# A fused linear-attention and MLP kernel: seven uneven MLP tiles (3, 4, 4, 4, 4, 3, 2) in place of six tiles of four, with an interleaved attention opening

## The chip, the cores and the metric

The kernel runs on one core of one Trainium2 chip. The metric is device time in microseconds (us) of one execution. An execution has a span (first to last instruction of the profile) and a measured time, which is 1.7 to 2.4 us longer than the span. A profile is one execution, so a few tenths of a us in it mean little; the medians of the timed runs decide.

Engine names: PE is TensorE (matmul), DVE is VectorE, ACT is ScalarE, POOL is GpSimd, SP is SyncE. POOL issues the loads, which also cast from 32-bit to 16-bit floats; SP issues the transposes that are done by DMA, and the stores.

## The reference, cut to what matters

There are 4 batches, 8 heads, 768 positions and head size 64. Decayed linear attention feeds an MLP with an ELU activation (512 to 2048 to 512) over 3072 tokens.

```python
# per batch and head, blocks of the sequence in order (lam: one decay per head)
intra = ((qb @ kb.T) * Dmask) @ vb              # Dmask[i,j] = lam**(i-j) for i >= j, else 0
inter = (qb * lam_pow) @ kv_state
out   = intra + inter
kv_state = lam**block * kv_state + (kb * rev_pow).T @ vb
# then, on x = out as [3072, 512]
h = x @ w_in                                    # 512 -> 2048
g = where(h > 0, h, exp(min(h, 0)) - 1)
y = g @ w_out                                   # 2048 -> 512
```

## The kernel before

The reference goes in blocks of 64 positions; the kernel, which computes the same sums, uses blocks of 128 tokens, called chunks here: 24 chunks, numbered 0 to 23, six for each batch. A *tile* is the set of chunks that go through the MLP together: four chunks, 512 tokens. A tile takes 16 *slots*, one for each 128 of the 2048 features: `mm1` gives 128 features for the tile's tokens, ACT and DVE make the ELU, and two slots later `mm2` adds the slot into one PSUM bank for each chunk. Slots are numbered through the whole kernel, so slot 16 is the first one of the second tile.

The attention of the chunks of the next tile is spread over the slots of the current one. Each chunk needs its queries and keys transposed, to have the head size on partitions. Chunks 0 to 3 have nothing to hide behind: their attention runs before slot 0, and they are transposed on PE; all later chunks are transposed by DMA.

```python
CPT = 4                                   # chunks in a tile
def att_T_dma(g):                         # transposes by DMA, issued on SP
    qt = asb.tile([128, NHP, 128], FP16, tag="qT", bufs=3, ...)
    z = asb.tile([128, NHP, 2, 128], FP16, tag="kz", bufs=3, ...)
    nc.sync.dma_start_transpose(out=qt[:], in_=...)        # queries
    nc.sync.dma_start_transpose(out=z[:]..., in_=kn[g % NB]...)   # keys, padded with zeros
def att_T_pe(g):                          # transposes on PE, only for chunks 0 to 3
    pt = ps.tile([128, 2, NHP, 128], FP16, tag="psH", bufs=2, ...)
    ...
def mm1(s):
    pH = ps.tile([128, MT], FP32, tag="psH", bufs=2, ...)
    for kk in range(NHP):
        nc.tensor.matmul(pH[:], lhsT=wi[:, kk, ...], rhs=xt[m][:, kk, :], ...)
    nc.scalar.activation(e[:], pH[:], AF.Exp)
    nc.scalar.activation(r[:], pH[:], AF.Relu)
def elu(s, e, r):                         # DVE, two inputs in SBUF
    nc.vector.scalar_tensor_tensor(out=g[:], in0=e[:], scalar=-1.0, in1=r[:], op0=ALU.add, op1=ALU.min)
def F(g):                                 # the slot in which chunk g's attention starts
    t, c = divmod(g, CPT)
    return 2 + 3 * c if t == 1 else (t - 1) * NFT - 2 + 4 * c
...
    if g < 2 * CPT:                       # chunks 4 to 7
        prep.append((f - 4, lambda g=g: att_T_dma(g)))
        prep.append((f - 1, lambda g=g: att_kd(g)))
    else:                                 # POOL scales q and k, then the transposes
        prep.append((f - 6, lambda g=g: (att_q(g), att_kd(g), att_T_dma(g))))
...
for g in range(CPT):                      # opening: chunk after chunk
    att_T_pe(g); att_ev(g); ...
    for hp in range(NHP):
        att_SU(g, hp)                     # scores and state, one bank for a pair of heads
        att_P(g, hp)                      # times the mask
    ...
```

Names in the profile: `psH` is the result of `mm1`, `psM` are the banks of `mm2`, `psSU` the scores, `psT` the PE transposes; `qn`, `kf`, `kn` and `vz` are the loaded queries, keys, zero-padded keys and values; `qT` and `kz` are transposed queries and keys; `kd` are decayed keys, `st` the state, `osb` the output before its store, `wi` and `wo` the weight slices.

## Time and profile before

| | before |
|---|---|
| time, median of 3 | 249.99 us (248.77 to 250.59) |
| span of the profile | 248.6 us |
| first `mm1` (slot 0) | 38.0 us |
| first `mm1` of the second tile (slot 16) | 79.5 us |
| last `mm1` to the end | 9.3 us |

The first lines of the profile page give the span, and the busy share of each engine in tenths, in 40 equal slices of 6.2 us. PEclk is the granted TensorE clock in tenths of full speed.

```profile
span 248.6 us, 3981 instructions
PE   0256658989697999999999999999999999999991
PEclk9999765999889999999999999999999999999999
```

From the 14th slice to the last but one PE is 90% busy or more. There is little to win there unless PE gets less to do. The loss is in the first 80 us and the last 10. The list of PE's waits (engine, what was to start, what released it: total, times, longest, in us) says what it waited for.

```profile
...
PE psH_507 L346 <- DVE xt_312 L333: 2.3, 1, 2.3
PE psSU_0_837 L270 <- DMA kz_692<-kn_92: 2.3, 1, 2.3
```

Those above them are waits for the first load and within the opening. The first shown is the end of the opening, at slot 0. The second is in the first tile: chunk 7's scores wait for its keys, transposed by DMA. The timeline (start, duration, engine, line, what; in brackets the idle time before and its releaser) has both, and the first `mm1` of slot 16 and the last of all.

```profile
38.01 1.87 PE L346 MATMUL psH_507<-xt_312,wi_0_127 128*128 128x512 f16 x4 [2.33 <-DVE xt_312 L333]
66.41 0.28 PE L270 MATMUL psSU_0_837<-qT_691,kz_692 128*128 128x128 f16 x2 [2.26 <-DMA kz_692<-kn_92]
79.52 1.03 PE L346 MATMUL psH_991<-xt_672,wi_0_127 128*128 128x512 f16 x4
239.26 1.03 PE L346 MATMUL psH_3072<-xt_2493,wi_4_131 128*128 128x512 f16 x4
```

How long a DMA transpose takes from issue to landing, in the last column, is told by the view of DMA issues: the keys of chunk 4, the first that is transposed by DMA, and those of chunk 7, which PE waited for.

```profile
kz_499<-kn_89 SPq DMA_TRANSPOSE x1, 10.5
...
kz_692<-kn_92 SPq DMA_TRANSPOSE x1, 8.9
```

And the chain of waits, followed back from the end, shows what leads to chunk 7's wait (start, duration, what).

```profile
19.62 8.68 DMA wi_2_129<-in_moe_w_in_dram
28.59 17.55 DMA qn_187<-in_q_dram
46.42 10.98 DMA kn_92<-in_k_dram
57.49 8.87 DMA kz_692<-kn_92
```

### The profile page before, as it was taken

The numbers are of one execution on the slowest core, as the hardware profiler recorded it, in microseconds if no ns is written. First come the engines' busy times: TensorE is split into PE (matmuls) and PEld (weight loads), VectorE is DVE, ScalarE is ACT, GpSimd is POOL, SyncE is SP. The second block draws the span as 40 slices with busy tenths as digits, with TensorE's granted clock in tenths as the row PEclk, the third lists the DMA queues.
The fourth block names the chain that finished last, engine by engine and source line by source line (L and its number), as shares of the span: only waits on it lengthen the run. The fifth ranks groups of instructions, "written<-read, shape, count | busy, mean of one in ns | idle before, by whom it ended". The sixth has DMA issues, their size and how long they took to land.

```text
span 248.6 us, 3981 instructions
## 1 busy us (share of the span) xinstructions
PE 215.2 (87%) x1344; PEld 113.0 (45%) x1344; DVE 166.2 (67%) x378; ACT 141.7 (57%) x307; POOL 117.0 (47%) x141
## 2 busy tenths in 40 slices
PE   0256658989697999999999999999999999999991
PEld 0144433545254455555555554555555555444440
DVE  8447764777468988665888987557888765444342
ACT  2794443545433756667666567576675665755651
POOL 7997534538999987802689868012400000000000
PEclk9999765999889999999999999999999999999999
DMA  6999999999999999982999999943227000040004
GB/s 43 125 151 182 191 112 192 169 176 124 149 151 158 129 262 159 88 84 52 179 171 143 123 104 127 177 83 63 44 70 186 3 0 1 0 171 0 0 0 169
DMA packets 115588, 28.05 MB, mean 113 GB/s; under 512 B 107888, under 2 KB 112496, under 8 KB 115568
## 3 DMA queue, kind: packets, MB, share of 16 engines
q0 software_dynamic: 79968, 13.64, 82.0%
q1 hardware_dynamic: 35600, 14.17, 31.2%
q8 instruction: 10, 0.16, 0.3%
q14 instruction: 10, 0.08, 0.1%
HBM read 27.27 MB, written 6.29 MB: 135 GB/s over the span
## 4 chain that ended last, share of the span: by engine, by line
PE 65%; DMA 19%; POOL 7%; DVE 3%; issue 2%; ACT 1%; DVEq 0%; SPq 0%; ACTq 0%; POOLq 0%
DMA qn_187<-in_q_dram 7%; DMA kn_92<-in_k_dram 4%; DMA kz_692<-kn_92 4%; DMA wi_2_129<-in_moe_w_in_dram 3%; PE psM_3_1558 L372 1%; PE psM_1_2506 L372 1%; PE psM_1_1556 L372 1%; PE psM_3_2508 L372 1%; PE psM_2_1557 L372 1%; PE psM_2_2507 L372 1%; PE psM_3_2042 L372 1%; PE psM_1_2040 L372 1%; PE psM_3_1087 L372 1%; PE psM_1_1085 L372 1%; PE psM_0_2505 L372 1%
## 5 line engine op out<-in xcount | busy, mean ns | idle before, releaser
L346 PEld LDWEIGHTS <-wi_4_131 128*128 128x128 f16 x96 | 9.4, 100 | 10.8 <-issue 1.1
L346 PEld LDWEIGHTS <-wi_3_130 128*128 128x128 f16 x96 | 9.2, 98 | 10.1
L346 PEld LDWEIGHTS <-wi_2_129 128*128 128x128 f16 x96 | 9.1, 98 | 9.9
L346 PEld LDWEIGHTS <-wi_0_127 128*128 128x128 f16 x48 | 4.9, 106 | 7.9 <-issue 4.1
L346 PEld LDWEIGHTS <-wi_1_128 128*128 128x128 f16 x48 | 4.9, 102 | 7.2 <-issue 2.5
L101 POOL DMA_DIRECT2D kn_91<-in_k_dram x6 | 4.5, 757 | 5.8 <-DMA qn_180<-in_q_dram 3.5
L101 POOL DMA_DIRECT2D kn_92<-in_k_dram x6 | 4.5, 757 | 4.4 <-DMA wo_3_135<-in_moe_w_out_dram 2.5
L212 POOL TENSOR_TENSOR kd_2298<-kn_90,ks 128x512 f16<-128x512 f16 x1 | 1.0, 1045 | 11.4 <-PE psSU_3_2225 L275 11.4
L212 POOL TENSOR_TENSOR kd_1591<-kn_92,ks 128x512 f16<-128x512 f16 x1 | 1.0, 1045 | 10.8 <-PE psSU_3_1501 L275 10.8
L246 PE MATMUL psT_221<-ident_141,qn_137 128*128 128x128 f16 x4 | 0.6, 308 | 4.9 <-DMA qn_137<-in_q_dram 4.9
L101 POOL DMA_DIRECT2D kn_90<-in_k_dram x6 | 4.5, 757 | 0.6 <-DMA wo_1_133<-in_moe_w_out_dram 0.4
L270 PEld LDWEIGHTS <-kz_0_93 128*128 128x128 f16 x16 | 1.6, 116 | 7.1 <-ACT kz_0_93 L257 7.1
L101 POOL DMA_DIRECT2D kn_89<-in_k_dram x6 | 4.6, 798 | 0.0
L270 PEld LDWEIGHTS <-kz_1_94 128*128 128x128 f16 x16 | 1.7, 120 | 5.3 <-ACT kz_1_94 L257 5.3
L101 POOL DMA_DIRECT2D vz_77<-in_v_dram x3 | 2.7, 900 | 2.8 <-DMA wo_4_136<-in_moe_w_out_dram 2.8
L270 PE MATMUL psSU_0_248<-qT_230,kz_0_93 128*128 128x128 f16 x2 | 0.6, 288 | 4.0 <-ACT kz_0_93 L257 4.0
L351 ACT ACTIVATE e_512<-psH_507 128x512 f32<-128x512 f32 x1 | 0.6, 597 | 5.9 <-PE psH_507 L346 5.9
L346 PE MATMUL psH_507<-xt_312,wi_0_127 128*128 128x512 f16 x4 | 1.9, 622 | 2.3 <-DVE xt_312 L333 2.3
L317 PEld LDWEIGHTS <-vz_83 128*128 128x128 f16 x24 | 2.4, 102 | 3.2 <-issue 0.6
L212 POOL TENSOR_TENSOR kd_2411<-kn_91,ks 128x512 f16<-128x512 f16 x1 | 1.0, 1045 | 5.7 <-issue 5.7
L317 PEld LDWEIGHTS <-vz_82 128*128 128x128 f16 x24 | 2.4, 98 | 2.8
L317 PEld LDWEIGHTS <-vz_81 128*128 128x128 f16 x24 | 2.3, 98 | 2.8
(1647 smaller groups left out, 851.0 us busy)
## 6 DMA issues: line engine op xcount, KB each, us to landing
wi_2_129<-in_moe_w_in_dram POOLq DMA_DIRECT2D x1, 512.0 KB, 8.7
wo_2_134<-in_moe_w_out_dram POOLq DMA_DIRECT2D x1, 512.0 KB, 10.7
wi_3_130<-in_moe_w_in_dram POOLq DMA_DIRECT2D x1, 512.0 KB, 14.0
wo_3_135<-in_moe_w_out_dram POOLq DMA_DIRECT2D x1, 512.0 KB, 16.6
wi_4_131<-in_moe_w_in_dram POOLq DMA_DIRECT2D x1, 512.0 KB, 12.5
wo_4_136<-in_moe_w_out_dram POOLq DMA_DIRECT2D x1, 512.0 KB, 15.0
vz_77<-in_v_dram POOLq DMA_DIRECT2D x3, 128.0 KB, 7.1
vz_78<-in_v_dram POOLq DMA_DIRECT2D x3, 128.0 KB, 5.5
```

What stands on the lines that cost most here:

```text
L101: nc.gpsimd.dma_start(out=dst, in_=src[:, rows].rearrange("h p d -> p h d"))
L212: eng.tensor_tensor(out=kd[:].rearrange("p (g t) d -> p g t d", t=2), in0=nats[g][1], in1=ks[:].rearrange("p (g t) -> p g t", t=2).unsquee ...
L246: nc.tensor.transpose(pt[:, j, hp, :], in_=src[:, 2 * hp : 2 * hp + 2, :], identity=ident16[:])
L270: nc.tensor.matmul(pu[:, hh * 128 : (hh + 1) * 128], lhsT=z[:, hp, hh, :], rhs=qt[:, hp, :], start=True, stop=True,)
L317: nc.tensor.matmul(po[:, hp, :], lhsT=vt[:, b0 : b0 + 2, :], rhs=P[:, hh, :], start=(hh == 0), stop=(hh == 1 and cb == 0), skip_group_chec ...
L346: nc.tensor.matmul(pH[:], lhsT=wi[:, kk, j * 128 : (j + 1) * 128], rhs=xt[m][:, kk, :], start=(kk == 0), stop=(kk == NHP - 1),)
L351: nc.scalar.activation(e[:], pH[:], AF.Exp)
L372: nc.tensor.matmul(psM[m][i][:], lhsT=g[:, i * 128 : (i + 1) * 128], rhs=wo16[wof[n][0]][:, wof[n][1], :], start=(n == 0), stop=(n == NFT ...
```

## The change

The intent is to start the MLP earlier and to end it sooner. The first tile has three chunks, so one chunk less is to be computed before slot 0; the last has two, so the last activations and stores are shorter. The opening's attention is interleaved: transposes of the next chunk, scores of this one and outputs of the last stand beside each other, four heads share a score bank, and the mask multiplication takes four heads at once. Zeroing is moved behind the front of the opening. Chunks 3 to 6, whose attention runs in the first tile, are transposed on PE. The DMA transposes of chunks 4 to 6 leave the queues. The weights come in eight slices of two slots in place of 2, 2, 4, 4, 4, and the order of the loads is another: chunk 7's load stood behind the last weight slice and now stands before slice 4 (slices are numbered from 0).

```diff
-    CPT = 4
-    MT = CPT * L
-    NMT = (B * S) // MT
+    TILES = [3, 4, 4, 4, 4, 3, 2]
+    NMT = len(TILES)
+    MTMAX = max(TILES) * L
+    T0 = [sum(TILES[:i]) for i in range(NMT + 1)]
+    G1 = T0[1]
+    G2 = T0[2]
...
-    WG = [2, 2, 4, 4, 4]
+    WG = [2] * 8
...
+    for g, (ft, f) in zip(range(G1, G2), ((-1, 1), (3, 5), (7, 9))):
+        at(ft, lambda g=g: (att_T_pe(g), att_ev(g)))       # chunks 3, 4, 5: on PE
+        regular(g, f)
+        prep.append((f - 1, lambda g=g: att_kd(g, nc.vector)))
+    at(12, lambda: (att_T_pe(G2 - 1), att_ev(G2 - 1)))      # chunk 6
+    short(G2 - 1, 13)
+    START = {4: (-2, 4), 3: (0, 5), 2: (2, 6)}              # first slot and step by tile size
+    for t in range(2, NMT):
+        off, step = START[TILES[t]]
+        for c in range(TILES[t]):
+            g, f = T0[t] + c, (t - 1) * NFT + off + step * c
+            regular(g, f)
+            prep.append((f - 6, lambda g=g: (att_q(g), att_kd(g, nc.gpsimd), att_T_dma(g))))
+            prep.append((f - 16, lambda g=g: emit_load(g)))
...
-    for g in range(CPT):
-        att_T_pe(g)
-        att_ev(g)
-        ...
+    att_T_pe(0)
+    att_ev(0)
+    late_zeros()
+    att_T_pe(1)
+    SU(0)
+    att_kd(0, nc.scalar)
+    ...
+    att_ev(1)
+    att_T_pe(2)
+    SU(1)
+    ...
```

A consequence: the chunks of the first two tiles have their queries scaled by DVE when the attention output is written, and these tiles now end at chunk 6. So chunk 7, the first of the third tile, is now the first to have its queries and keys scaled by POOL, and the first to be transposed by DMA. Its attention starts in slot 14.

## The prediction

> **What bounds it now.** From about 80 us on, TensorE does: the chain of waits shows one mm1 group (four matmuls, 0.86 us) every 2.06 us while attention is interleaved, every 1.73 us in the last tile, PE 100% busy in the windows. So one chunk-slot of the MLP (a 128-token chunk, one of 16 feature slots) costs 1.73/4 = 0.43 us and an attention chunk 4 x 0.33 = 1.3 us of PE. Their sum does not change. Losses are at the ends. Opening: the first mm1 starts at 38.0 us (timeline), after a serial attention of four chunks (first scores at 10.7, 17.3, 24.2, 31.2). Tile 0: slots 0 to 16 take 38.0 to 79.7 = 41.7 us; the PE sum is 16 x 1.73 + 4.5 x 1.3 = 33.5. The rest is a cold clock (windows: 0.50 from 33 to 42 us), a 2.3 us wait for the DMA-transposed keys of chunk 7 (landed 66.4 us, 8.9 after issue), a cold clock again, and 1 us waits on the one score bank. A cold clock after a gap is what the Trainium skill says (TensorE: Matmul & The Clock Gate, Part 1). Tail: last mm1 at 239.3, end 248.6.
>
> **What the change does.**
> 1. Opening: one chunk less (about 6.9 us), interleaved, wider masks (0.69 us for four heads instead of 2 x 0.42), DVE zeroing off the front. Adding durations on DVE (13 us of work after the first transposed copy at about 9 us) and ACT (15 us) gives the first mm1 at 25.5 us (24 to 28).
> 2. Tile 0 has three chunks: 16 x 1.29 = 21 us, attention of four chunks (5), eight PE transposes for each (0.45 warm): 28 us warm, 30 with a cold start.
> 3. PE transposes free the DMA queues of 1.2 MB in the opening and take 8 to 10 us of latency off chunks 3 to 6. Weight slices land in time by my sum (the queue moved 145 GB/s on q/k/v, 200 on weights): slice 4 at 37, slice 7 at 48 us.
> 4. New wait: chunk 7 is now the first with a DMA transpose, needed in slot 14, about 52 us. On POOL its q scaling stands behind the loads of chunks 8 and 9, whose issue waits for slice 7 (eight loads outstanding). So the transposes issue at about 50 us and land at 57 to 59: PE waits some 6 us and restarts cold. Slot 16 starts about 63 us instead of 79.7.
> 5. After slot 16: 21 instead of 20 chunks of MLP (+6.9), one more attention chunk (+1.3), one more tile change (+0.6), tail with two chunks (shorter activations, two stores instead of four: -2.1): 168.9 + 6.7 = 175.6 us.
>
> **Sum.** Span 63 + 175.6 = 238.6; timed runs are 1.4 us above: **240.0 us**, range 234.5 to 244.5. Chances: faster by over 2% 0.93, within 2% 0.06, slower 0.01.
>
> **What would show it.** First mm1 near 25.5 us; slots of 1.75 us in tile 0; a PE wait of 4 to 8 us for the transposed keys of chunk 7 near 52 to 58 us, then a clock of 0.5; slot 16 near 63; last mm1 to end 7.2 us instead of 9.3; 2.06 us unchanged in full tiles.
>
> **What would make it wrong.** No wait for chunk 7 (shorter transpose latency): 233 to 235 us. Weights or chunk 6 late in tile 0, or chunk 7's load held by the zeroing of its key buffer, which ACT does last in the opening: 243 us or more. In the last tiles ACT or the two activation banks could bind at 0.86 us a slot.

## The result, and the profile after

The changed kernel gives correct results and takes 243.67 us (median of 4, 243.32 to 243.78) against 249.73 of the kernel before. The ratio is 0.976, with a 95% interval of 0.972 to 0.979. Ratios here are the mean time of one kernel's runs over that of the other's runs of the same rounds, so they are not quite the ratio of the medians that are quoted. Executions over 1.5% slower than the fastest of the same kernel are left out of the means. The change is faster by 2.4%. The predicted 240.0 was 3.7 us too low; the time lies within the range.

| profile | before | predicted | after |
|---|---|---|---|
| span | 248.6 | 238.6 | 241.3 |
| slot 0, first `mm1` | 38.0 | 25.5 | 25.8 |
| wait for chunk 7's keys | 2.3 | about 6 | 5.9 |
| slot 16, first `mm1` | 79.5 | 63 | 64.4 |
| from there to the end | 169.1 | 175.6 | 176.9 |
| last `mm1` to the end | 9.3 | 7.2 | 6.8 |

The first lines of the page, after; a slice is 6.0 us.

```profile
span 241.3 us, 4272 instructions
PE   1377799960989999999999999999999999999992
PEclk9999999996799999999999999999999999999999
```

PE is busy much earlier, but has a hole in the tenth slice, and the clock is low after it. PE's waits, after, name the hole: the same wait for chunk 7's keys as before, 2.6 times as long.

```profile
PE psSU_0_885 L333 <- DMA kz_671<-kn_92: 5.9, 1, 5.9
...
PE psT_217 L260 <- DMA qn_151<-in_q_dram: 2.9, 1, 2.9
...
PE psM_1_1026 L436 <- DVE osb_1_990 L444: 1.1, 1, 1.1
```

The timeline, after: slot 0, the end of the wait, the `mm1` of slot 15 at half the clock (1.49 us, where that of slot 14, of the same width, took 0.81), slot 16, and the last `mm1`.

```profile
25.79 0.81 PE L409 MATMUL psH_442<-xt_302,wi_0_118 128*128 128x384 f16 x4
59.87 0.39 PE L333 MATMUL psSU_0_885<-qT_670,kz_671 128*128 128x128 f16 x2 [5.88 <-DMA kz_671<-kn_92]
61.44 1.49 PE L409 MATMUL psH_898<-xt_302,wi_7_125 128*128 128x384 f16 x4
64.39 1.03 PE L409 MATMUL psH_937<-xt_583,wi_0_118 128*128 128x512 f16 x4
234.51 0.60 PE L409 MATMUL psH_3280<-xt_2905,wi_7_125 128*128 128x256 f16 x4
```

In the view by stretches (stretch; length; busy time of PE, PEld, DVE, ACT, POOL; then the granted clock, the DMA share and GB/s) the clock falls during the wait and stays at 0.50 to about 63 us. The Trainium skill, page "TensorE: Matmul & The Clock Gate", Part 1, says that the clock is half after about one idle window of 3.4 us, and comes back after about as long a busy one. This trace agrees in the return: PE is busy again from 59.87 us, and in stretches of 0.5 us the clock is 0.50 up to 63.0 and 1.00 from 63.5. The fall came sooner than that: PE's last matmul before the wait ended at 54.0 us, and the clock is 0.93 in the stretch from 56.0 and 0.50 from 56.5, so it fell after some 2.4 us.

```profile
54.00:57.00 3.00, 0.00 (x0) 0.00 (x0) 0.62 (x2) 1.14 (x6) 3.00 (x5) 0.90 1.24 113
57.00:60.00 3.00, 0.13 (x2) 0.13 (x3) 0.00 (x0) 0.00 (x0) 3.00 (x4) 0.50 2.23 155
60.00:63.00 3.00, 3.00 (x13) 1.50 (x12) 1.45 (x4) 0.00 (x0) 3.00 (x4) 0.50 1.35 144
```

Why were the keys late? The chain of waits, after, has it (most pieces are left out; nearly all of them are loads that POOL issues).

```profile
26.18 8.80 DMA vz_82<-in_v_dram
...
41.25 8.73 DMA wo_7_133<-in_moe_w_out_dram
50.02 0.49 issue
50.51 0.88 POOL vz_78 L108
51.41 1.06 POOL qn_409 L233
52.47 1.00 POOL kd_668 L225
...
53.88 5.95 DMA kz_671<-kn_92
```

POOL's work stands in the trace in the order of the program. Its scaling of chunk 7's queries (`qn_409`) stands behind the loads of chunks 8 and 9, and the last of those (`vz_78`) waited for the last weight slice (`wo_7`, issued at 41.25) to land; the late loads in this trace each wait for the landing of the load eight places before them. Only then come the scaling, the decayed keys, and the transposes on SP. So up to about 60 us the chain of the kernel after is mostly its queue of loads, as that of the kernel before was.

### The profile page after: what moved, and what is told of

It reads as the page before. It is cut to its first block, busy times and chain, and to the rows that moved or that the text cites. A ratio compares the mean times of both kernels' runs of the same rounds, so it can differ in the third digit from the quotient of the medians.

```text
span 241.3 us, 4272 instructions
## 1 busy us (share of the span) xinstructions
PE 212.7 (88%) x1444; PEld 120.5 (50%) x1444; DVE 164.8 (68%) x381; ACT 147.6 (61%) x335; POOL 121.1 (50%) x146
## 4 chain that ended last, share of the span: by engine, by line
PE 67%; DMA 13%; POOL 10%; DVE 5%; issue 3%; ACT 1%; SPq 0%; DVEq 0%; ACTq 0%; POOLq 0%
DMA vz_82<-in_v_dram 4%; DMA wo_7_133<-in_moe_w_out_dram 4%; DMA wo_1_127<-in_moe_w_out_dram 4%; DMA kz_671<-kn_92 2%; PE psM_3_1503 L436 1%; PE psM_1_1026 L436 1%; PE psM_1_2416 L436 1%; PE psM_3_2418 L436 1%; PE psM_1_1501 L436 1%; PE psM_2_1502 L436 1%; PE psM_2_2417 L436 1%; PE psM_2_1027 L436 1%; PE psM_0_1500 L436 1%; PE psM_3_1028 L436 1%; PE psM_0_2415 L436 1%
## 5 line engine op out<-in xcount | busy, mean ns | idle before, releaser
L409 PEld LDWEIGHTS <-wi_7_125 128*128 128x128 f16 x56 | 5.7, 102 | 6.3 <-issue 0.9
L409 PEld LDWEIGHTS <-wi_1_119 128*128 128x128 f16 x56 | 5.3, 97 | 6.7 <-issue 2.1
L409 PEld LDWEIGHTS <-wi_3_121 128*128 128x128 f16 x56 | 5.4, 98 | 5.3
L409 PEld LDWEIGHTS <-wi_5_123 128*128 128x128 f16 x56 | 5.4, 98 | 5.3
L409 PEld LDWEIGHTS <-wi_4_122 128*128 128x128 f16 x56 | 5.4, 98 | 5.0
L409 PEld LDWEIGHTS <-wi_2_120 128*128 128x128 f16 x56 | 5.3, 98 | 4.8
L409 PEld LDWEIGHTS <-wi_6_124 128*128 128x128 f16 x56 | 5.3, 98 | 4.8
L409 PEld LDWEIGHTS <-wi_0_118 128*128 128x128 f16 x56 | 5.3, 98 | 4.7
L414 ACT ACTIVATE e_903<-psH_898 128x384 f32<-128x384 f32 x1 | 0.5, 490 | 7.8 <-PE psH_898 L409 7.8
L108 POOL DMA_DIRECT2D kn_92<-in_k_dram x6 | 4.5, 764 | 0.8 <-DMA wi_2_120<-in_moe_w_in_dram 0.6
L374 PEld LDWEIGHTS <-vz_79 128*128 128x128 f16 x24 | 2.6, 112 | 2.8 <-issue 0.9
L333 PEld LDWEIGHTS <-kz_671 128*128 128x128 f16 x8 | 0.7, 114 | 6.1 <-DMA kz_671<-kn_92 6.1
L374 PEld LDWEIGHTS <-vz_84 128*128 128x128 f16 x24 | 2.3, 98 | 2.8 <-DVE xt_583 L395 0.5
L374 PEld LDWEIGHTS <-vz_81 128*128 128x128 f16 x24 | 2.3, 98 | 2.5
L374 PEld LDWEIGHTS <-vz_80 128*128 128x128 f16 x24 | 2.3, 98 | 2.5
L374 PEld LDWEIGHTS <-vz_82 128*128 128x128 f16 x24 | 2.3, 98 | 2.5
```

The costliest lines, as they stand in the source:

```text
L108: nc.gpsimd.dma_start(out=dst, in_=src[:, rows].rearrange("h p d -> p h d"))
L333: nc.tensor.matmul(pu[:, hh * 128 : (hh + 1) * 128], lhsT=z[:, hp, hh, :], rhs=qt[:, hp, :], start=True, stop=True,)
L374: nc.tensor.matmul(po[:, hp, :], lhsT=vt[:, b0 : b0 + 2, :], rhs=P[:, hh, :], start=(hh == 0), stop=(hh == 1 and cb == 0), skip_group_chec ...
L409: nc.tensor.matmul(pH[:, :w], lhsT=wi[:, kk, j * 128 : (j + 1) * 128], rhs=xt[m][:, kk, :w], start=(kk == 0), stop=(kk == NHP - 1),)
L414: nc.scalar.activation(e[:, :w], pH[:, :w], AF.Exp)
```

## The experiments

Each was run beside the kernel before on the same chip, on four chips. "After" is the changed kernel; diffs are against it. Slot 16 is the start of its first `mm1`. Twelve kernels ran; all gave correct results.

The theory is that (1) the wait for chunk 7's transposes, which stands at the end of POOL's queue of loads, hides most of what the opening wins; (2) taking the transposes of chunks 3 to 6 off the DMA queues is the largest part of the gain; (3) the short last tile is worth some 2 us; (4) the eight weight slices are worth little. The main rival is that the earlier opening itself is the gain, and chunk 7's wait just one wait among several. The experiments test one part of it, the interleaving; the other part, that one chunk less stands before slot 0, was never undone alone.

### 0. The changed kernel again (after_again)

No edit.

> Control: the changed kernel, unedited, on the chip of this call. Both theories: 243.7 us as before (243.3 to 244.1), PE wait of 5.9 us for the DMA-transposed keys of chunk 7.

Measured: 243.43 us (243.35 to 244.4), ratio 0.975 (0.972 to 0.979), span 241.3. The median repeats to 0.1%. But the six runs of one kernel can lie 3 us apart (oldopen below), so a difference of 1 us between medians is at the limit of what can be read.

### 1. Chunk 7's scaling and transposes early (early7)

```diff
-            prep.append((f - 6, lambda g=g: (att_q(g), att_kd(g, nc.gpsimd), att_T_dma(g))))
+            at_q = 1.5 if g == G2 else f - 6          # chunk 7: in slot 2 instead of 8
+            prep.append((at_q, lambda g=g: (att_q(g), att_kd(g, nc.gpsimd), att_T_dma(g))))
```

Chunk 7 also gets its own buffers for `qT` and `kd`, so that the early work waits for no buffer.

> Edit: chunk 7's q scaling, decayed keys and DMA transposes are recorded before the loads of chunks 8 and 9 (own buffers), so POOL reaches them at about 42 us instead of 51.4. Theory (the 5.9 us wait comes from POOL's program order, and the cold restart after it costs about 1.6 us more): keys of chunk 7 land at about 50 to 52, the wait in slot 14 (54 us) is gone; but chunk 8's transposes keep their place (issue 57.8, landing 64.6) and are needed at about 62 us, so some 2 to 3 us of wait come back there: 238 to 240 us. Rival A (the keys only hide another limit of tile 0, such as DVE, ACT or the load queue): under 2 us gained, 242 or more.

Measured: 241.84 us (241.15 to 242.75), ratio 0.969 (0.965 to 0.972), span 239.8. Slot 16 starts at 58.5 us, 5.9 earlier than after, as the theory wants. But the time fell by only 1.8 us. PE's waits between 56 and 72 us tell where the rest went.

```profile
PE psSU L335 <- DMA kz<-kn: 3.4, 1, 3.4
```

This wait ends at 66.8 us and is chunk 8's: its transposes were issued at 58.4 and 59.7 us, at about the same time as in the kernel after (57.8 and 59.1), while PE now needs them some 6 us sooner. The wait was moved on to the next chunk. The expected size was a miss.

### 2. The same, and the loads behind it in a better order (early7_ord)

```diff
-            prep.append((f - 16, lambda g=g: emit_load(g)))
+            prep.append((-2 if g == G2 else f - 13, lambda g=g: emit_load(g)))
```

The edit of early7 stays in. The loads of chunk 8 and later are recorded three slots later, so that POOL's scaling no longer stands behind the loads of the chunks after.

> Edit: as early7, and the loads from chunk 8 on are recorded three slots later, so that each chunk's q scaling on POOL stands before the load of the chunk two further. Theory: the wait moves to nothing: about 7.5 us less than the changed kernel, 236 us (235 to 237.5), no PE wait over 1.5 us between 30 and 70 us, clock 1.0 there. Rival A: 241 or more. Rival B (the whole gain was had by early7): same time as early7 within 0.5 us.

Measured: 237.93 us (236.82 to 239.38), ratio 0.953 (0.949 to 0.957), span 234.7. Slot 16 is at 57.9 us, and from there to the end it takes 176.8 us, the 176.9 of the kernel after. (The profiled run was the fastest of the six, 236.82 us.) No wait for a transpose is left. So the chunk 7 wait, with the order of POOL's queue that makes it, costs the changed kernel 243.67 - 237.93 = 5.7 us (5.5 against after_again on the same chip): nearly as much as the whole change had won. That part of the theory is shown.

It was 1.9 us above the expectation. The timeline of DVE around 40 us shows a new loss: the ELU instruction `g`, which takes 0.56 us, takes 2.86.

```profile
38.93 0.56 DVE L424 SCALAR_TENSOR_TENSOR g<-e,r 128x384 f16<-128x384 f32 x1
40.54 2.86 DVE L424 SCALAR_TENSOR_TENSOR g<-e,r 128x384 f16<-128x384 f32 x1
```

The timeline of POOL shows what ran meanwhile: the two multiplications for chunk 7.

```profile
40.92 1.06 POOL L234 TENSOR_TENSOR qn<-qn,qp 128x512 f16<-128x512 f16 x1
41.92 1.05 POOL L226 TENSOR_TENSOR kd<-kn,ks 128x512 f16<-128x512 f16 x1
```

The Trainium skill, page "SBUF — State Buffer", section "Who interferes with whom", says: "A DVE instruction with two SBUF inputs contends with a GpSimd instruction that reads SBUF". `g` has two SBUF inputs, and both POOL multiplications read SBUF; the trace agrees, with 2.86 us for 0.56. The time from slot 9's `mm1` to slot 10's is 3.14 us here and 1.58 in the kernel after. Experiment 5 tests it.

### 3. The old opening in the changed kernel (oldopen)

The opening is written as in the kernel before, chunk after chunk with a score bank for a pair of heads, but for three chunks; all else is as after.

```diff
+    for g in range(G1):
+        att_T_pe(g)
+        att_ev(g)
+        ...
+        att_kd(g, nc.scalar)
+        ...
+        if g > 0:
+            PIs(g - 1)
+            att_X(g - 1)
+        pu = [old_S(g, hp) for hp in range(NHP)]
+        for hp in range(NHP):
+            old_st(g, hp, pu[hp])
```

> Edit: only the opening undone: chunks 0 to 2 one after the other with one narrow score bank per head pair, all else as changed. Theory (the first mm1 is off the critical path, because the wait for chunk 7's keys absorbs it): first mm1 about 4 to 5 us later (30 to 31 us), slot 14 reached at about 58 instead of 54, the wait for chunk 7 about 2 us instead of 5.9, time within 1 us of the changed kernel (243 to 245). Rival C (an earlier first mm1 is worth its full time): 4 to 5 us slower, 248 us.

Measured: 242.1 us (240.34 to 243.48), ratio 0.969 (0.964 to 0.974), span 239.1; the intervals of this ratio and of the changed kernel's overlap. So the interleaved opening gains nothing that can be seen in the changed kernel. The six runs fall into two groups, 240.3 to 241.1 and 243.1 to 243.5 us, and the profile is of the faster one; why is open. In it the `mm1` of slot 0 starts 2.5 us later (28.25 against 25.79; the line shown holds slots 0 and 1), yet slot 16 comes 2 us sooner, at 62.4.

```profile
28.25 2.76 PE L402 MATMUL psH<-xt,wi 128*128 128x384 f16 x8
...
59.51 0.28 PE L326 MATMUL psSU<-qT,kz 128*128 128x128 f16 x2 [0.67 <-DMA kz<-kn]
```

Chunk 7's keys land at nearly the same time whichever opening is used (the wait ends at 59.51 us, after at 59.87). PE arrives there later, so it waits 0.67 us in place of 5.88, and the clock is not as low for as long: 0.77 and 0.66 in the stretches from 54 to 60 us, and 1.00 from 60 on, where the kernel after has 0.50 to 63 us. Here an earlier start by interleaving only meant waiting longer and restarting cold.

### 4. Old opening, with the wait taken away (oldopen_early7_ord)

The edits of 2 and 3 together.

> Edit: the old serial opening (as in oldopen) together with early7_ord, so without the wait for chunk 7's keys. In oldopen the first mm1 came only 2.4 us later than in the changed kernel, and the time did not grow. Theory (the opening counts once nothing behind it waits): 2 to 2.5 us slower than early7_ord, 240 us. Rival D (tile 0 is paced by the load queue in any case, so the opening never counts): within 0.5 us of early7_ord, 238 us.

Measured: 240.89 us (239.5 to 240.94), ratio 0.965 (0.962 to 0.968), span 237.6, slot 16 at 60.2 us. Beside early7_ord this is 3.0 us slower in the medians, 2.3 us in slot 16's start, and the ratios' intervals are apart. So the interleaved opening is worth 2 to 3 us as soon as the wait for chunk 7 is gone, and nothing that can be seen before. As far as the interleaving goes, the rival falls. It stays open for the larger part of the earlier start: with the old way of writing the opening, slot 0 is still at 28.25 us and not at 38.0, because one chunk less stands before it (and zeroing is moved).

### 5. Chunk 7 without POOL's arithmetic (c7raw)

Chunk 7 is treated like chunks 3 to 6: its queries are scaled when the attention output is evicted by DVE, its keys are decayed on DVE. Its load moves back, from before weight slice 4 to behind slice 5 (in front of chunk 6's), and its transposes are by DMA, early.

```diff
-            if g < G2:
+            if g <= G2:
...
+            if g == G2:
+                prep.append((1.5, lambda g=g: att_T_dma(g)))
+                prep.append((f - 1, lambda g=g: att_kd(g, nc.vector)))
+                continue
...
+        (-2, lambda: emit_load(G2)),          # before weight slice 6
```

The later loads are recorded at f - 13, as in early7_ord.

> Edit: chunk 7's q is not scaled on POOL but, like chunks 0 to 6, at the product's eviction on DVE; its decayed keys are made on DVE; its load stands after slice 5; later loads as in early7_ord. So POOL does no tensor work before chunk 8. In early7_ord one g instruction on DVE (two SBUF inputs) took 2.86 us instead of 0.56, just while POOL did its two multiplications at 40.9 to 43.0 us, and slots 9 to 10 took 3.1 us instead of 1.6. Theory F (DVE and POOL wait for each other at the SBUF port; the skill says so for a DVE instruction with two SBUF inputs): no g over 1.3 us before 50 us, slot 16 near 56 us instead of 57.9, 236 us (235 to 237). Rival G (the long slot is the weight queue's doing): slots 9 to 10 stay at 3 us, 237.5 or more.

Measured: 239.11 us (238.96 to 239.93), ratio 0.960 (0.957 to 0.962), span 238.1: a miss, 1.2 us slower than early7_ord in the medians (the intervals of the ratios just touch). On the disputed point it was plain: with no POOL arithmetic there, the `g` at the same place takes its usual time.

```profile
40.32 0.56 DVE L423 SCALAR_TENSOR_TENSOR g<-e,r 128x384 f16<-128x384 f32 x1
```

Slots 9 to 10 take 1.58 us again. So POOL's multiplications did stretch it. But the moved load and the transposes now stand beside the load of chunk 6, and PE waits for that one twice. PE's waits for DMA from 26 to 75 us (the last is for chunk 8's transposes, at 66.4 us):

```profile
PE psT L261 <- DMA kf<-in_k_dram: 1.8, 1, 1.8
PE psSU L340 <- DMA vz<-in_v_dram: 1.2, 1, 1.2
PE psSU L334 <- DMA kz<-kn: 1.0, 1, 1.0
```

In early7_ord PE waits for no DMA in this stretch. These 4 us are more than the 1.6 us that were won.

### 6. Another plan of tiles, ending with four (tail4)

```diff
-    TILES = [3, 4, 4, 4, 4, 3, 2]
+    TILES = [3, 4, 3, 3, 3, 4, 4]
```

This was meant to measure the short last tile alone.

> Edit: only TILES, to [3,4,3,3,3,4,4]: seven tiles and the same work, but the last tile has four chunks as before the change. Theory (a two-chunk tail saves what its shorter activations and two fewer stores save): last mm1 to the end 9.3 us instead of 6.8, 2.5 us slower than the changed kernel: 245.9 us (245 to 247). Rival H (the size of the last tile only moves work about): within 0.7 us of 243.5.

Measured: 239.94 us (239.27 to 240.63), ratio 0.962 (0.960 to 0.965), span 237.8. It was to be slower and was 3.7 us faster. The end is slower, as expected: 9.6 us from the last `mm1` to the end, against 6.8. But the third tile now has three chunks, and in the change's own table of starts (`START`) a tile of three begins its attention at slot 16 and not at 14. That moves chunk 7's preparation two slots later, and the loads of chunks 8 and 9 three and four: its transposes are issued at 49.7 and 51.1 us, before chunk 9's load, in place of 52.5 and 53.9, and they are needed later. The wait for chunk 7 is gone. The edit changed two things, so as a measure of the tail it failed; it is a second, unplanned sign of what the wait costs, though the plan changes later tiles as well.

### 7. The same third tile, with a short end (tiles343)

```diff
-    TILES = [3, 4, 4, 4, 4, 3, 2]
+    TILES = [3, 4, 3, 4, 4, 4, 2]
```

> Edit: only TILES, to [3,4,3,4,4,4,2]. As in tail4 the third tile has three chunks, so chunk 7 is needed in slot 16 instead of 14 and its scaling on POOL stands before the load of chunk 9; the last tile has two chunks as in the changed kernel. In tail4 this took the wait for chunk 7 away (slot 16 at 54.7 us instead of 64.4), which hid what its four-chunk tail cost (last mm1 to the end 9.6 us in the trace, 6.8 in the changed kernel). Theory: tail4's 239.9 less 2.8 us: 237.1 us (236.3 to 238.2). Rival H (the size of the last tile only moves work about): 239.9 within 0.7 us.

Measured: 237.61 us (236.93 to 238.51), ratio 0.952 (0.948 to 0.956), span 236.0. Against tail4 this is 2.3 us, and in the profiles the time from the last `mm1` to the end is 7.05 us against 9.6. So the two-chunk end is worth about 2.3 us, as the prediction had it (2.1). The two plans differ in the middle tiles too, so the 2.55 us between the ends in the profiles are the cleaner figure. The line of a list of seven numbers gives as much as the reordering of experiment 2.

### 8. Chunks 3 to 6 transposed by DMA again (dmaT, dmaT2)

```diff
-        at(ft, lambda g=g: (att_T_pe(g), att_ev(g)))
+        prep.append((f - 4, lambda g=g: att_T_dma(g)))
...
-    at(12, lambda: (att_T_pe(G2 - 1), att_ev(G2 - 1)))
+    prep.append((7.5, lambda: att_T_dma(G2 - 1)))       # dmaT: 9
```

The keys of these chunks are loaded into the zero-padded form, in two halves each. This undoes more than the change did: chunk 3 was transposed on PE before, too, and four more loads stand in POOL's queue.

> Edit: only the PE transposes of chunks 3 to 6 undone: they are transposed by DMA again, four slots ahead, everything else as changed. Theory (the PE transposes pay by taking 1.5 MB and their latency out of the load queue): chunk 3's keys land near 31 us instead of being ready at 27; slice 7 lands 6 to 8 us later, and with it chunk 7's transposes at about 66 us; time about 6 to 7 us more than the changed kernel, 250 us (247 to 252). Rival I (they were hidden, prepared four slots ahead): within 1 us of 243.5.

Measured for dmaT: 259.15 us (257.17 to 259.7), ratio 1.038 (1.034 to 1.042). This edit was flawed: chunk 6's transposes were recorded behind chunk 7's on SP, which waits for POOL, and PE waited 14.5 us for them. The mended one puts them ahead.

> Edit: as dmaT, with its slip mended: there chunk 6's DMA transposes stood behind chunk 7's on the one issuing queue, which waited for POOL, and PE waited 14.5 us for them. Now they stand before. Theory (the PE transposes pay by taking 1.5 MB and 8 to 10 us of latency out of the opening): waits of 5.8 us for chunk 3 and about 3 us for chunk 5 stay, slice 7 and so chunk 7's transposes come 6 to 8 us later than in the changed kernel: 250 us (247 to 253). Rival I (hidden): within 1.5 us of 243.5.

Measured for dmaT2: 254.75 us (252.8 to 256.45), ratio 1.021 (1.016 to 1.026), span 252.9, 11.1 us slower than after. From slot 16 on it takes 176.8 us as ever; the loss is all before it (slot 16 at 76.1 us in place of 64.4). PE's waits:

```profile
PE psSU L335 <- DMA kz<-kn: 14.2, 5, 7.0
...
PE psH L411 <- DMA wi<-in_moe_w_in_dram: 2.6, 1, 2.6
```

The transposes are late five times (for chunks 3 to 7: 1.8, 0.8, 3.1, 7.0 and 1.5 us), and a weight slice once. The last weight slice was issued at 50.6 us against 41.3 after, and POOL's scaling of chunk 7 came at 60.7 against 51.4: the loads are held back too, by the transposes, by the split key loads or by both. On PE, eight transposes of a warm chunk took 0.45 us (39.46 to 39.91 us in the kernel after). So transposing chunks 3 to 6 on PE is worth 11 us in the changed kernel, the largest effect of any experiment; with DMA it is slower than the kernel before (by a ratio of 1.021). What the change's own part of it is worth, chunks 4 to 6 and with the same key loads, was not measured apart.

### 9. The old weight slices (slices5)

```diff
-    WG = [2] * 8
+    WG = [2, 2, 4, 4, 4]
```

> Edit: only the weight slices undone, to five of 2, 2, 4, 4, 4 feature groups, in the same order among the loads. Theory (at most eight loads are outstanding, and slices land some 2 us before their slot): the same bytes in fewer and larger loads, slices 4 to 7 not waited for; time within 1 us of the changed kernel's 243.5, the wait for chunk 7's keys still 5 to 7 us. Rival J (smaller slices let the MLP start on a half-landed slice): a PE wait for a slice of 2 us or more in slots 4 to 12, and 2 us or more slower.

Measured: 242.39 us (241.22 to 243.38), ratio 0.971 (0.967 to 0.975), span 240.8. PE waited for no slice, and 5.0 us for chunk 7's keys. The eight slices give nothing here.

### 10. A version meant to beat both (best)

Tiles as in tiles343, chunk 7 scaled as in c7raw, but with its transposes right behind its own load, which stays where it was; later loads at f - 13.

```diff
+            if g == G2:
+                prep.append((f - 16, lambda g=g: (emit_load(g), att_T_dma(g))))
+                prep.append((f - 1, lambda g=g: att_kd(g, nc.vector)))
+                continue
...
-            prep.append((f - 16, lambda g=g: emit_load(g)))
+            prep.append((f - 13, lambda g=g: emit_load(g)))
```

> Tile plan of tiles343 (3,4,3,4,4,4,2), and chunk 7 treated like chunks 0 to 6: its queries are scaled at the eviction and its keys decayed on DVE, so POOL has no tensor work for it; its transposes stand right behind its own load on the SP queue. Theory (POOL's multiplications stretch DVE's two-input instructions and delay the change of tile): about 1 us below tiles343's 237.6, so 236.5 us (235.5 to 237.5), slot 16's first mm1 at 54.5 to 55.4 us in the profile, and the PE wait at the change of tile, 1.67 us in tiles343, under 1. Rival (as in c7raw, the transposes moved next to loads cost as much as the POOL work did): within 0.5 us of tiles343, or slower, with PE waits on DMA over 0.8 us before slot 16.

Measured: 237.45 us (236.91 to 239.31, 6 runs), ratio 0.952 (0.949 to 0.956), span 234.7. That is the rival's number: 0.2 us from tiles343, and the intervals are nearly the same. The wait at the first change of tile did shrink (0.8 us, 1.7 in tiles343), and before slot 16 PE no longer waits for a DMA once it has begun the first tile. But DVE's timeline has the stretched `g` again, 2.98 us at 50.8, and POOL's timeline has two multiplications beside it (the first of them is shown; the second ends at 53.4 us). They are now chunk 8's, which come earlier, as POOL no longer has chunk 7's before them and takes the later loads behind them.

```profile
50.84 2.98 DVE L423 SCALAR_TENSOR_TENSOR g<-e,r 128x384 f16<-128x384 f32 x1
```

```profile
51.31 1.09 POOL L233 TENSOR_TENSOR qn<-qn,qp 128x512 f16<-128x512 f16 x1
...
```

Taking chunk 7's share off POOL handed its place to chunk 8's. Three versions end within 0.5 us of each other, at 237.5 to 237.9. Of these, tiles343 is the one to keep: it changes one line.

| kernel | median, us | ratio to before | slot 16, us |
|---|---|---|---|
| after | 243.67 | 0.976 | 64.4 |
| early7 | 241.84 | 0.969 | 58.5 |
| early7_ord | 237.93 | 0.953 | 57.9 |
| oldopen | 242.1 | 0.969 | 62.4 |
| oldopen_early7_ord | 240.89 | 0.965 | 60.2 |
| c7raw | 239.11 | 0.960 | 60.1 |
| dmaT2 | 254.75 | 1.021 | 76.1 |
| slices5 | 242.39 | 0.971 | 63.9 |
| tail4 (other plan) | 239.94 | 0.962 | 54.7 |
| tiles343 (other plan) | 237.61 | 0.952 | 55.4 |
| best (other plan) | 237.45 | 0.952 | 56.0 |

In the last three, slot 16 can't be compared with the others: chunk 7's attention starts in slot 16 and not in 14, so less work lies before it.

## Why the prediction was right or wrong

Faster by more than 2% was right, and the time lies in the range. It was right for most of its reasons; the sum was 3.7 us too low. Point by point:

- **What bounds the kernel: right.** From slot 16 to the end takes 176.7 to 176.9 us in after, early7_ord, oldopen, dmaT2 and slices5, whose first tiles differ by up to 18 us. (It takes more where a wait lies behind slot 16: 181.3 us in early7, 178.0 in c7raw.) The ends are what can be changed.
- **Slot 0 at 25.5 us: right in size (25.8), in part by luck.** The first transposed copy, counted at about 9 us, was done at 7.5, and PE then waited 2.9 us for chunk 1's queries to load, which the sum did not have. The two errors cancel in part.
- **The opening as a gain: not thought through.** Step 1 gives a time for slot 0, but the sum rests on step 4, where slot 16 follows from the end of the wait. What was not said is that the interleaving of step 1 is then worth nothing: experiment 3 shows that it wins nothing in this kernel, and experiment 4 that it wins 2 to 3 us when the wait is gone. The one chunk less of step 1 was not tested.
- **PE transposes: right in direction.** The prediction had the mechanism in its step 3, but no figure for what it is worth in all. Undoing it for chunks 3 to 6 cost 11 us (dmaT2), which includes chunk 3 and the split key loads.
- **Chunk 7's wait: right.** Predicted some 6 us, ending at 57 to 59, with a cold restart; measured 5.9, ending at 59.9, with the clock at 0.50. That the length agrees so well is in part luck: both ends came later than said, the start by some 2 us (54.0 for about 52), as the slots from 2 to 14 took 2.0 us in the mean and not 1.75. Its cause is as told (POOL's scaling behind loads, which wait for slice 7 to land). The last slice landed at 50.0 us, not 48.
- **Slot 16 at 63 us: 1.4 us too early,** which is the later end of the wait and the rest of the cold stretch.
- **From slot 16 on, 175.6 us: 1.3 us too small.** One more tile change was counted as 0.6 us; the first one waited 1.1 us for DVE's output copy. The end was better than counted, 6.8 us and not 7.2, and tiles343 against tail4 shows the term (2.3 us). Most of the 1.3 us is in PE work that the sum had too small: between the first `mm1` of slot 16 and the last `mm1` PE was busy 167.65 us, against 158.05 before, so 9.6 us more where the sum had 8.2. Which instructions these are was not traced further.
- **Timed runs 1.4 us above the span: 1.0 us too small.** The median was 2.4 us above it here. The figure is the distance from one profiled span of the kernel before to the median of its runs; that execution's own time (250.35) was 1.75 above its span. The other 0.6 us is that each run of the changed kernel lies 2.3 to 2.4 us above its own span; why is not known.

1.4, 1.3 and 1.0 make the 3.7 us.

- **"No wait for chunk 7: 233 to 235 us": too low.** Three kernels have no such wait and take 237.5 to 237.9. Most of this can be the same 2.3 us of the last two points. Beside them stands the stretched `g`: when POOL's arithmetic runs on time, it runs beside DVE's `g`. The stretching is shown; what it costs in the whole time is not, as c7raw, which removes it, lost more by its loads.
- **What would make it wrong (zeroing of chunk 7's key buffer by ACT holding its load): did not happen.** The load was issued at 28.5 us, after waiting 0.6 us for a weight slice to land.
- **The eight slices in time: right,** and slices5 shows that five would have done.

## What to carry to other kernels

Before costing an earlier start, look at which engine's queue releases the first late wait: if it is the queue of loads, as here, part of an earlier start only makes that wait longer, and may add a cold clock. Work that a transfer needs (here a scaling on POOL) should not stand in the same queue behind loads that are not urgent; an earlier scaling with a three-slot shift of the loads, or another list of tile sizes, won nearly as much again as the whole change. And when a wait is taken away, look for the next one on the same path, and for what now runs beside what: here a stretched DVE instruction, then the next chunk's.

## What the Trainium skill lacked or had wrong

- Page "DMA: Bandwidth & Descriptors", section "Latency and other measured facts", has a bandwidth for transposes by DMA (261 GB/s with a non-contiguous middle dimension, more for contiguous ones), but no latency beside other traffic. A key transpose here moves 128 x 1024 elements of 2 bytes, 262 KB, so by that figure it would take 1.0 us (an estimate). In the kernel before, beside the loads, it took 10.5 us from issue to landing in the opening and 8.9 in the first tile, and 6.0 for chunk 7's in the kernel after. What it costs the rest of the queue is also missing: four chunks of transposes, with their split key loads, moved the last weight slice's issue by 9.4 us (50.6 against 41.3).
- Page "SBUF — State Buffer", section "Who interferes with whom", says that `g` and POOL's multiplications contend, and the traces agree. It gives no duration for such a pair: 0.56 us became 2.86 and 2.98. Its section "SBUF: two separate sides" also says that whichever starts first has the shared ports for its whole instruction. In early7_ord the record of `g` starts at 40.54 and the first multiplication's at 40.92, yet `g` ends after the second one (43.40 against 42.97); best shows the same order. Records of POOL are rough, so this is a doubt and not a proof.
- Page "TensorE: Matmul & The Clock Gate", Part 1, names an idle window of about 3.4 us for the half clock. In the kernel before, a wait of 2.3 us (64.1 to 66.4 us) was enough: the clock was 0.50 in the stretch from 67 to 70 us. In stretches of 0.5 us it fell at 67.0 us, and in the kernel after at about 56.4; PE was busy for 1.1 and 1.0 us of the 3.4 us before. So in both the stretch before the fall was not wholly idle.

```profile
67.00:70.00 3.00, 3.00 (x12) 1.30 (x10) 1.37 (x4) 0.13 (x1) 2.82 (x5) 0.50 2.52 137
```

- The same page, Part 4, gives about 275 ns as the duration of a transpose on PE within a kernel, but no pace for several back to back. Issued back to back in a stretch with the clock at 1.00, eight took 0.45 us here, so the pace is 56 ns (39.46 to 39.91 us of the kernel after).
